# Two 57x64 blocks a score tile for the second half of the heads, u's first stage in 64-row halves, and a new written-out order

## The chip, the cores and the metric

The kernel runs on one core of a Trainium2 chip. The metric is the device time of one execution in microseconds. An execution's span, in the profile, goes from the first to the last instruction; the execution's own time is a little longer. The engines are PE (TensorE's matmuls, with their weight loads as PEld), DVE (VectorE), ACT (ScalarE), POOL (GpSimd) and SP, which here issues most DMAs. Each works through its own queue in order.

## The reference

Inputs are bf16; S = 2048 positions, D = 640 channels, H = 32 heads of 20. The result is a gated sum of two branches.

```python
x = A_q
g = sigmoid((x * gate_w).sum(-1, keepdims=True))
# A: a 4-tap causal filter on k, times v, then a causal convolution over all S positions by FFT
kv = k_shift * v
y  = irfft(rfft(kv, 2*S) * rfft(ssm_k, 2*S))[:S] + kv * ssm_D
a  = q * y
# B: attention of each position to the 8 positions 0, 2, .., 14 behind it
idx = pos[:, None] - 2 * arange(8)[None, :]
o = softmax(mask(q . k[idx] * scale)) . v[idx]
b = o @ wo
out = g * a + (1 - g) * b
```

## The kernel before

**Order.** Every part of the kernel is a Python generator (a stream) that yields one request at a time: a PE unit that takes PSUM, an eviction on ACT or DVE, a DMA on SP, something on POOL. The string `ORDER` names the stream that goes next, one letter a request (with `-`, the other of the two engines that a request allows). So all five instruction queues are written out by hand in one table; the waits between engines follow from the data. PSUM is four double banks; a unit takes one or two of them, and its eviction gives them back.

**Attention.** Positions are split into even and odd ones, so the 8 keys of a query are neighbours. A parity has 9 blocks of `BQ` = 114 queries, with `BK` = 121 keys each: 18 blocks. Four heads share a step t (8 steps), in four 32-row strips of `kb` and `qb`, which hold 20 features and 11 mask rows that push scores outside the band far down. `score_gen` makes scores with keys on partitions and queries on columns (L647, a 31x128 weight tile and 114 columns), and ACT takes the exponential of two heads and 3 or 4 blocks at a time out of PSUM into `ETall` (L658), a ring of `NET` = 9 tiles. `pv_gen` multiplies (L682): the weights are `ETall`, the moving side is V with a column of ones (`VW`), 21 columns a head; three heads are streamed (63 columns) though only the first counts, the next matmul overwrites the rest. DVE divides by the sum (L692, L694) and writes to `oS`, which lies in `VW`. From t = 6 on some pad matmuls (L652) follow the scores. `vproj` makes V (L526), half of the heads each; `qkproj` makes q and k (L573), which reach `kb` and `qb` by DMA.

**Convolution.** Two halves P of the channels, 40 channels a group of partitions. `transform` runs for h (the kernel) and u (k times v, in the tile `vin`, made by `conv` and `conv_v` on DVE): ten units of a first stage (`s1_unit`; h has two 64-row matmuls of 128 columns a channel, L713; u has one 128-row matmul of 256 columns against a block diagonal matrix, L709), each evicted as 1024 columns, then eleven units of a second stage (`s2_unit`, L732), evicted in place as 960 or 640 columns. u's tile `UC` is allocated (`u_slot`) where attention's buffers lay, so u's first stage starts when attention is done. `swaps` makes, by DMA, a copy `Hw` of h with the halves of the partitions exchanged: per P four steps of two DMAs, each step after a tiny POOL copy (L822) that waits until the step before has landed. `products` multiplies u with h and with `Hw` on DVE (L764, 44 instructions), `inverse1` is the inverse's first stage (L843), `final` its second (L930).

**End.** `op_tr` transposes `oS` (L861, 18 a unit, 5 units) into `oT`, which takes `vin`'s place; `outproj` multiplies it with `wo` (L877), 32 units; ACT scales them by 1 - g into `bl` (L891); DVE puts everything together and SP writes it out. The evictions of all stages go through `copy` (L244 on ACT, L246 on DVE).

Of the kernel before, what the change touches and what calls it, by code (L numbers as in the profile page):

```python
# [27 lines left out]
BK = 121  # L28
NBP = 9
# [10 lines left out]
NET = 9  # L40
GROUPS = [[0, 1, 2, 3], [4, 5, 6, 7], [8, 9, 10, 11], [12, 13, 14], [15, 16, 17]]
PARTS = [((0, 1, 2), 0, 2), ((3, 4), 12, 1)]
# [174 lines left out]
def kernel(  # L217
# [41 lines left out]
    ident = p0.tile([128, 128], BF, name="ident")  # L259
    F = p0.tile([128, 512], BF, name="F")  # L260
# [30 lines left out]
    ETall = pR.tile([128, NET, 2, 3 * BQ + 128], BF, name="ETall")  # L291
# [106 lines left out]
    def heads():  # L398
# [33 lines left out]
        nc.vector.memset(ETall[:, :, :, 3 * BQ:], 1.0)  # L432
        for q in range(4):
            nc.gpsimd.memset(kin[32 * q:32 * q + 1, 0:3, :], 0.0)
        for e in range(3):
            masks(e)

# [81 lines left out]
    def vproj(hp):  # L519
        for j in range(NBP):  # L520
            for par in range(2):
                g = yield Req("P", 0.0, xdeps(BQ * j - PRE, BQ * j - PRE + BK) + [ev(f"Wv{hp}")], take=1, half=1, pe=(5, 136.0, 272.0, 126.0))
                ps = psum(g)
                s0 = X0 + HP * par + BQ * j - PRE
                for dt in range(NDT):
                    nc.tensor.matmul(ps[0:BK, 0:320], lhsT=xT[:, dt, s0:s0 + BK], rhs=Wv[:, dt, 320 * hp:320 * hp + 320],  # L526
                                     start=(dt == 0), stop=(dt == NDT - 1))
                r = yield Req("AD", n=320, deps=[g.done], give=g.banks)
                copy(r.eng, VW[0:BK, NBP * par + j, 16 * hp:16 * hp + 16, 0:DH], ps[0:BK, 0:320].rearrange("p (h d) -> p h d", d=DH))
# [107 lines left out]
    def score_gen():  # L637
        s = 0
        for t in range(NT):
            kb, qb = ksets[t % 3], qsets[t % 3]  # L640
            for gi, blocks in enumerate(GROUPS):
                nb = len(blocks)
                g = yield Req("P", 0.0, [ev(f"set{t}")] + ([ev(f"near{t}")] if t < 2 else []), take=2, pe=(4 * nb, 11.8, 30.0, 11.8))
                for bb, b in enumerate(blocks):
                    for h4 in range(4):
                        r = 32 * h4
                        nc.tensor.matmul(psum(g, h4 // 2)[:, h4 % 2, BQ * bb:BQ * bb + BQ], lhsT=kb[r:r + DH + NF, BK * b:BK * b + 128],  # L647
                                         rhs=qb[r:r + DH + NF, BQ * b:BQ * b + BQ],
                                         start=True, stop=True, tile_position=(r, 0), skip_group_check=True)
                w = 512 - BQ * nb  # L650
                for n in range(0 if t < 6 else (2 if nb == 3 else (14 if t == 6 else 7))):
                    nc.tensor.matmul(psum(g, 1)[:, 1, BQ * nb:512], lhsT=mm[:, 0:128], rhs=mm[:, 0:w], start=True, stop=True, skip_group_check=True)  # L652
                if gi == len(GROUPS) - 1:
                    mark(f"sc{t}", g)
# [338 lines left out]
```

## Time and profile before

| | |
|---|---|
| time, 3 runs | 221.22 us median (220.27 to 222.21) |
| profiled execution | 219.82 us, span 218.0 us |
| mean granted TensorE clock | 0.990 |
| PE busy (modelled) | 205.2 us, 94% |
| DVE busy | 183.4 us, 84% |
| ACT busy | 173.5 us, 80% |
| DMA | 33.35 MB, mean 153 GB/s |

Matmuls are pipelined and their ends are modelled, so PE's busy share overstates how full PE is; how long a run of matmuls really holds PE is read from the chain of waits, which gives start and length of each run.

### The profile page before, as it was taken

How to read it: one execution, taken by the hardware profiler on the slowest of the kernel's cores; microseconds unless marked ns; L12 is line 12 of the kernel's file. 1: busy time of each engine (PE TensorE's matmuls, PEld its weight loads, DVE VectorE, ACT ScalarE, POOL GpSimd, SP SyncE). 2: the span in 40 equal slices, each digit the busy share in tenths (PEclk: the TensorE clock that was granted, in tenths of full speed). 3: DMA queues.
4: the chain of work that ended last, by engine and by line, in shares of the span. 5: the costliest groups of instructions: out<-in, count | busy, mean ns of one | idle time of the engine just before them, and what ended most of it. 6: DMA issues, size and time to landing. Idle time of an engine off the chain costs nothing.

```text
span 218.0 us, 8528 instructions
## 1 busy us (share of the span) xinstructions
PE 205.2 (94%) x3642; PEld 166.8 (76%) x3642; DVE 183.4 (84%) x264; ACT 173.5 (80%) x251; POOL 50.8 (23%) x129
## 2 busy tenths in 40 slices
PE   6999999999999999999997988999999999999990
PEld 3876987696677677656685766899888999998880
DVE  6647778997998998789897968998999997898782
ACT  0354387769998998989998988999899999487760
POOL 7980811460517045405420000000000000000000
PEclk9999999999999999999999699999999999999999
DMA  6999799699954993899984196767449064003544
GB/s 199 349 251 287 205 185 188 137 168 154 272 160 102 150 146 64 152 150 151 168 160 107 31 223 140 174 158 226 110 110 289 7 149 95 3 3 96 139 128 131
DMA packets 69049, 33.35 MB, mean 153 GB/s; under 512 B 51476, under 2 KB 66708, under 8 KB 69012
## 3 DMA queue, kind: packets, MB, share of 16 engines
q1 hardware_dynamic: 65684, 27.66, 62.0%
q0 software_dynamic: 2880, 4.90, 9.6%
q8 instruction: 28, 0.46, 1.0%
q10 hardware_dynamic: 448, 0.26, 0.4%
q14 instruction: 9, 0.07, 0.1%
HBM read 19.51 MB, written 2.62 MB: 102 GB/s over the span
## 4 chain that ended last, share of the span: by engine, by line
PE 66%; DVE 12%; ACT 6%; SPq 6%; DMA 5%; issue 3%; DVEq 0%; ACTq 0%
PE PS L573 16%; PE PS L526 12%; PE PS L877 10%; PE PS L843 8%; ACT ETall L658 5%; PE PS L682 5%; SPq L324 5%; PE PS L647 4%; PE PS L732 3%; DVE UC L246 3%; DMA h_lin<-in_A_ssm_k_dram 3%; DVE SX L246 3%; PE PS L930 2%; DMA WvT<-in_B_wqkv_dram 2%; PE PS L444 2%
## 5 line engine op out<-in xcount | busy, mean ns | idle before, releaser
L658 ACT ACTIVATE ETall<-PS 121x912 bf16<-121x912 f32 (+1 forms) x80 | 63.9, 865 | 6.4 <-PE PS L647 6.0
L573 PE MATMUL PS<-xT,Wqk 128*128 128x342 bf16 (+1 forms) x300 | 49.8, 310 | 0.7 <-ACT stg L244 0.3
L244 ACT CAST UC<-PS 128x1024 bf16<-128x1024 f32 (+2 forms) x49 | 44.4, 1030 | 4.0 <-DVE UC L246 3.1
L573 PEld LDWEIGHTS <-Wqk 128*128 128x128 bf16 x300 | 27.3, 97 | 14.6 <-issue 0.5
L526 PE MATMUL PS<-WvT,xT 128*121 128x320 bf16 x180 | 27.5, 301 | 0.6 <-DMA WvT<-in_B_wqkv_dram 0.3
L472 DVE TENSOR_TENSOR KX<-KX 128x1280 bf16<-128x1280 bf16 x32 | 25.3, 820 | 0.3
L526 PEld LDWEIGHTS <-xT 128*121 128x121 bf16 x180 | 23.5, 134 | 2.2 <-issue 0.4
L623 POOL DMA_DIRECT2D qb<-stg x29 | 14.5, 504 | 43.3 <-ACT stg L244 27.1
L877 PE MATMUL PS<-wo,oT 128*128 128x320 bf16 x160 | 24.5, 302 | 0.1
L244 ACT CAST stg<-PS 128x363 bf16<-128x363 f32 (+1 forms) x39 | 17.1, 472 | 8.5 <-PE PS L573 8.2
L877 PEld LDWEIGHTS <-oT 128*128 128x128 bf16 x160 | 21.0, 145 | 1.5 <-issue 0.5
L623 POOL DMA_DIRECT2D kb<-stg x36 | 18.0, 510 | 14.8 <-ACT stg L244 7.6
L732 PEld LDWEIGHTS <-G 64*128 64x128 bf16 x512 | 18.1, 93 | 3.8 <-issue 2.5
L682 PEld LDWEIGHTS <-ETall 121*128 121x128 bf16 x576 | 17.8, 97 | 1.6 <-issue 0.2
L682 PE MATMUL PS<-VW,ETall 121*128 121x63 bf16 (+2 forms) x576 | 18.5, 186 | 0.1
L843 PE MATMUL PS<-F,Hw 128*128 128x128 bf16 x160 | 18.1, 219 | 0.0
L843 PEld LDWEIGHTS <-Hw 128*128 128x128 bf16 x160 | 17.9, 114 | 0.0
L647 PE MATMUL PS<-qb,kb 31*128 31x114 bf16 x576 | 15.6, 212 | 2.3 <-ACT ETall L658 1.2
L246 DVE CAST UC<-PS 128x1024 bf16<-128x1024 f32 x13 | 15.3, 1220 | 2.6 <-ACT UC L244 1.2
L647 PEld LDWEIGHTS <-kb 31*128 31x128 bf16 x576 | 9.3, 93 | 10.3 <-issue 8.8
L246 DVE CAST SX<-PS 128x1024 bf16<-128x1024 f32 (+2 forms) x13 | 14.6, 1159 | 2.8 <-PE PS L732 1.7
L891 ACT ACTIVATE bl<-PS,omg 128x320 bf16<-128x320 f32 x30 | 15.4, 566 | 1.9 <-PE PS L877 1.4
(75 smaller groups left out, 329.9 us busy)
## 6 DMA issues: line engine op xcount, KB each, us to landing
xn<-in_A_q_dram SPq DMA_DIRECT2D x8, 320.0 KB
h_lin<-in_A_ssm_k_dram SPq DMA_DIRECT2D x16, 160.0 KB
vin<-in_A_v_dram SPq DMA_DIRECT2D x8, 320.0 KB
Hw<-H SPq DMA_DIRECT2D x8, 320.0 KB
q<-in_A_q_dram SPq DMA_DIRECT2D x8, 320.0 KB
Hw<-SX SPq DMA_DIRECT2D x8, 320.0 KB
kb<-stg POOLq DMA_DIRECT2D x28, 85.1 KB, 4.1
out_dram<-q SPq DMA_DIRECT2D x16, 120.0 KB
```

What stands on the lines that cost most here:

```text
L244: nc.scalar.copy(dst, src)
L246: nc.vector.tensor_copy(dst, src)
L472: eng.tensor_tensor(d, kin[:, n + 3 - j:n + 3 - j + m, :], w.to_broadcast([128, m, QC]), ALU.mult)
L526: nc.tensor.matmul(ps[0:BK, 0:320], lhsT=xT[:, dt, s0:s0 + BK], rhs=Wv[:, dt, 320 * hp:320 * hp + 320], start=(dt == 0), stop=(dt == NDT - 1))
L573: nc.tensor.matmul(ps[:, 0:n], lhsT=Wqk[:, dt, w, 128 * ft:128 * ft + 128], rhs=xT[:, dt, s0:s0 + n], start=(dt == 0), stop=(dt == NDT - 1))
L623: (nc.sync if near else nc.gpsimd).dma_start(dst[r0:r0 + rows, 0:wd], stg[fa - f0:fb - f0, 0:wd])
L647: nc.tensor.matmul(psum(g, h4 // 2)[:, h4 % 2, BQ * bb:BQ * bb + BQ], lhsT=kb[r:r + DH + NF, BK * b:BK * b + 128], rhs=qb[r:r + DH + NF, B ...
L658: nc.scalar.activation(ETall[0:BK, e, :, 0:BQ * nb], psum(g, k)[0:BK, :, 0:BQ * nb], ACT.Exp, scale=SCALE)
L682: nc.tensor.matmul(O[:, (b - b0) // 6, c0:c0 + 21 * nh], lhsT=ETall[0:BK, e, hh, BQ * bb:BQ * bb + 128], rhs=VW[0:BK, b, 4 * t + h4:4 * t ...
L732: nc.tensor.matmul(ps[:, c, 160 * jj:160 * jj + 160], lhsT=G[rows, j0 + jj, 64 - 64 * rr:192 - 64 * rr], rhs=Am[rows, rr].rearrange("p o ( ...
L843: nc.tensor.matmul(d, lhsT=st[(key, P)][:, c, o + il // 4, :, il % 4], rhs=M[:, k, :], start=(k == 0), stop=(k == 1), skip_group_check=True)
L877: nc.tensor.matmul(op, lhsT=oT[:, ft].rearrange("p h m a -> p a (h m)")[:, t, :], rhs=wo[:, ft, 320 * n:320 * n + 320], start=(ft == 0), s ...
```

## The change

What it does, in eight parts:

1. For steps t = 4 to 7 (`NEW` = 4) a block of 114 queries becomes two of `SQ` = 57 queries with `SK` = 64 keys each, one in the lower and one in the upper 64 partitions of the score tile. A score matmul has a 32x64 weight tile and 57 columns; there are twice as many, and an ACT exponential holds two heads and six blocks, 128x684. A step has three score groups in place of five, so 24 exponentials replace 40.
2. `pv_gen` for these steps has two matmuls a head and block, each with a 64x64 tile on the diagonal of the array and 21 columns.
3. `vproj` for the second half of the heads makes V in the same two row halves: two matmuls with a 128x64 tile in place of one with 128x121.
4. All exponentials are stored with 64 columns per 57 queries, so `ETall` has 8 tiles instead of 9. Fewer and wider pad matmuls stand behind the last scores (24, not 71).
5. u's first stage works as h's does: two 64-row matmuls of 128 columns a channel. For P = 0 it writes to a tile of its own, `UA`, which is there before attention ends; its second stage evicts from `UA` into `UC`.
6. `oT` moves into `UA`'s place, and the copy `Hw1` for P = 1 into `vin`'s place, so its swap now waits for u's first stage of both halves.
7. `op_tr` transposes against `pick`, a matrix that also drops the doubled rows, and has an extra transpose of 8 rows for each parity, 20 a unit.
8. `ORDER` is another table from the first third on.

```diff
-NET = 9
-GROUPS = [[0, 1, 2, 3], [4, 5, 6, 7], [8, 9, 10, 11], [12, 13, 14], [15, 16, 17]]
+NET = 8
+GROUPS = [[[0, 1, 2, 3], [4, 5, 6, 7], [8, 9, 10, 11], [12, 13, 14], [15, 16, 17]],
+          [[0, 1, 2, 3, 4, 5], [6, 7, 8, 9, 10, 11], [12, 13, 14, 15, 16, 17]]]
...
 ORDER = """
-dddii-iddifd-iifxdddxedidffdfddefcicccii-iddiedd-icddlie-iiiyf-yddccdixiyyfy-xe-ydddexixdxddyyfyy-xcccxxffccccccccciiiciiccdcii
+-iidddii-iddifd-iifxdddxedidffdfddefcicccii-iddiedd-icddlie-iiiyf-yddccdix-icydydcccfcccifceccfcccdcccccxyicyycixiedi-ydfd-xiciy
...
@@ vproj @@
+                    for i in range(2 if split else 0):
+                        nc.tensor.matmul(ps[SK * i:SK * i + SK, 0:320], lhsT=xT[:, dt, s0 + SQ * i:s0 + SQ * i + SK], rhs=rhs,
+                                         start=(dt == 0), stop=(dt == NDT - 1), tile_position=(0, SK * i), skip_group_check=True)
...
@@ score_gen @@
+                    for i in range(1 + split):
+                        for h4 in range(4):
+                            r = 32 * h4
+                            c, q = BK * b + SQ * i, BQ * b + SQ * i
+                            nc.tensor.matmul(psum(g, h4 // 2)[SK * i:SK * i + SK, h4 % 2, bw * bb:bw * bb + bw] if split else psum(g, h4 // 2)[:, h4 % 2, bw * bb:bw * bb + bw],
+                                             lhsT=kb[r:r + DH + NF, c:c + (SK if split else 128)], rhs=qb[r:r + DH + NF, q:q + bw],
+                                             start=True, stop=True, tile_position=(r, SK * i), skip_group_check=True)
-                for n in range(0 if t < 6 else (2 if nb == 3 else (14 if t == 6 else 7))):
+                for n in range(0 if t < 6 else (((5 if t == 6 else 3)) if split else (2 if nb == 3 else (14 if t == 6 else 7)))):
...
@@ pv_gen @@
-                                nh = min(3, 4 - h4)
+                                nh = min(1 if split else 3, 4 - h4)
+                                for i in range(1 + split):
+                                    rows = slice(SK * i, SK * i + SK) if split else slice(0, BK)
...
+                                                     start=True, stop=True, tile_position=(SK * i, SK * i), skip_group_check=True)
...
@@ s1_unit @@
-            if whole:
-                nc.tensor.matmul(ps[:, il // 2, 256 * (il % 2):256 * (il % 2) + 256], lhsT=vin[:].rearrange("p c n i -> p i (c n)")[:, i], rhs=F1d,
-                                 start=True, stop=True, skip_group_check=True)
-            for qp in range(0 if whole else 2):
+            for qp in range(2):
                 rows = slice(64 * qp, 64 * qp + 64)
+                lhsT = vin[rows].rearrange("p c n i -> p i (c n)")[:, i] if key == "u" else h_lin[rows, i - PL * P, :, :].rearrange("p c n -> p (c n)")
...
@@ transform @@
-        Am = st[(key, P)]
+        early = key == "u" and P == 0
+        Am = st["UA"] if early else st[(key, P)]
...
+        if early:
+            yield Req("N", 0.0, [ev("p3")])
+        Bm = st[(key, P)]
...
@@ swaps @@
-            yield Req("N", 0.0, outs("h", P) + [ev("p2")])
+            yield Req("N", 0.0, outs("h", P) + ([ev("us10"), ev("us11")] if P else [ev("p2")]))
...
@@ op_tr @@
-            for b in range(NB):
-                par, j = b // NBP, b % NBP
-                w = min(BQ, HS - BQ * j)
-                nc.tensor.transpose(tr[:, par, BQ * j:BQ * j + w], oS[0:w, b, 128 * ft:128 * ft + 128], ident[0:w, 0:w])
+            for par in range(2):
+                for j in range(NBP - 1, -1, -1):
...
+                    nc.tensor.transpose(tr[:, par, q:q + k], oS[0:k, NBP * par + j, feats], pick[0:k, c:c + k])
+                nc.tensor.transpose(tr[:, par, BQ:BQ + 8], oS[0:8, NBP * par + 1, feats], ident[0:8, 0:8])
```

How the order moves work shows at three places. Lines have other numbers in the changed kernel: the exponential is L680, `copy` L248 and L250, the swaps L859.

On ACT, from the last third of attention to the first evictions of the outer projection, before (`SX` is h of P = 1, `UC` is u, `ETall` the exponentials, `bl` the projection):

```order
L658 ACTIVATE ETall<-PS 121x2x456 x6
L244 CAST SX<-PS 128x2x512 x4
L658 ACTIVATE ETall<-PS 121x2x342 x4
L658 ACTIVATE ETall<-PS 121x2x456 x6
L658 ACTIVATE ETall<-PS 121x2x342 x4
L244 CAST SX<-PS 128x80x12 x4
L244 CAST UC<-PS 128x2x512 x12
L244 CAST UC<-PS 128x80x12 x11
L891 ACTIVATE bl<-PS,omg 128x320 x2
```

The same place on ACT in the changed kernel:

```order
L680 ACTIVATE ETall<-PS 128x2x6x57 x4
L248 CAST H_301<-PS 128x80x12
L248 CAST SX<-PS 128x2x512
L680 ACTIVATE ETall<-PS 128x2x6x57 x2
L248 CAST UA<-PS 128x2x512
L680 ACTIVATE ETall<-PS 128x2x6x57 x2
L248 CAST SX<-PS 128x2x512
L680 ACTIVATE ETall<-PS 128x2x6x57 x2
L248 CAST SX<-PS 128x2x512 x2
L248 CAST UA<-PS 128x2x512
```

The exponentials are fewer, h's second half is less far when they end, and u's first stage (`UA`) stands partly among them; the rest of it follows mixed with h's stages.

On SP, from the last swap of P = 0 on, before (`Hw` are the swaps of h, `wo` the outer projection's weights, the second `SX` the table T, q the gated input):

```order
L904 DMA q_2428<-in_A_q_dram 32x8x640
L828 DMA Hw<-H_289 64x5x512 x2
L828 DMA Hw<-SX 64x5x512 x2
L324 DMA wo<-in_B_wo_dram 128x5x640
L828 DMA Hw<-SX 64x5x512 x6
L324 DMA SX<-cf_T 128x4x512 x2
```

And in the changed kernel:

```order
L859 DMA Hw_2980<-H_301 64x5x512 x7
L329 DMA wo<-in_B_wo_dram 128x5x640
L859 DMA Hw_2980<-H_301 64x5x512
L859 DMA Hw_3695<-SX 64x5x512 x8
L938 DMA q_3370<-in_A_q_dram 32x8x640 x3
```

`wo` now stands ahead of the last swap of P = 0, all eight swaps of P = 1 behind it, and every load of q behind the swaps.

On PE, `op_tr` between two parities, before:

```order
L861 MATMUL PS<-ident,VW 128x114
L861 LDWEIGHTS VW
L861 MATMUL PS<-ident,VW 128x112
L861 LDWEIGHTS VW
L861 MATMUL PS<-ident,VW 128x114
```

And in the changed kernel:

```order
L894 LDWEIGHTS VW
L894 MATMUL PS<-pick,VW 128x121
L895 LDWEIGHTS VW
L895 MATMUL PS<-ident,VW 128x8
L894 LDWEIGHTS VW
L894 MATMUL PS<-pick,VW 128x120
```

A transpose of 8 rows now stands between transposes of up to 122 rows; in the built program its tile is 32 rows by 128 columns, while that of its neighbours is 128 by 128.

More of the change, by code (lines that the diff above doesn't have):

```diff
@@ L28 @@
 BK = 121
+SQ = 57
+SK = 64
+NEW = 4
 NBP = 9
@@ L259 @@
     ident = p0.tile([128, 128], BF, name="ident")
+    pick = p0.tile([128, 3 * BK], BF, name="pick")
     F = p0.tile([128, 512], BF, name="F")
@@ L290 @@
         ksets.append(kb); qsets.append(qb)
-    ETall = pR.tile([128, NET, 2, 3 * BQ + 128], BF, name="ETall")
+    ETall = pR.tile([128, NET, 2, 8 * SK], BF, name="ETall")
     rds = []
@@ L431, in heads @@
             nc.gpsimd.memset(xT[:, :, X0 + HP * c + HS:X0 + HP * (c + 1)], 0.0)
-        nc.vector.memset(ETall[:, :, :, 3 * BQ:], 1.0)
+        nc.vector.memset(ETall[:].rearrange("p e h (c q) -> p (e h c) q", q=SK)[:, :, SQ:], 1.0)
         for q in range(4):
@@ L436, in heads @@
             masks(e)
+        runs, c = [(0, SQ), (SK, SQ), (SQ, 7)], 0
+        for k in (BK + 1, HS - BQ * (NBP - 1) + 8):
+            runs += [(SQ, 7), (k - 1, 1), (0, SQ), (SK, k - SK - 1)]
+        for r, w in runs:
+            nc.gpsimd.tensor_copy(pick[:, c:c + w], ident[:, r:r + w])
+            c += w
     def xpose():
@@ L640, in score_gen @@
             kb, qb = ksets[t % 3], qsets[t % 3]
-            for gi, blocks in enumerate(GROUPS):
+            split = t >= NEW
+            bw = SQ if split else BQ
+            for gi, blocks in enumerate(GROUPS[split]):
                 nb = len(blocks)
-                g = yield Req("P", 0.0, [ev(f"set{t}")] + ([ev(f"near{t}")] if t < 2 else []), take=2, pe=(4 * nb, 11.8, 30.0, 11.8))
+                g = yield Req("P", 0.0, [ev(f"set{t}")] + ([ev(f"near{t}")] if t < 2 else []), take=2, pe=(4 * nb * (1 + split), 11.8, 30.0, 11.8))
@@ L658, in score_gen @@
-                    nc.scalar.activation(ETall[0:BK, e, :, 0:BQ * nb], psum(g, k)[0:BK, :, 0:BQ * nb], ACT.Exp, scale=SCALE)
+                    r = yield Req("A", 68.0 + 0.834 * 2 * bw * nb, [g.done, etfree[e], ev("ET")], give=[g.banks[k]])
+                    nc.scalar.activation(ETall[0:rows, e].rearrange("p h (c q) -> p h c q", q=SK)[:, :, 0:bw * nb // SQ, 0:SQ],
+                                         psum(g, k)[0:rows, :, 0:bw * nb].rearrange("p h (c q) -> p h c q", q=SQ), ACT.Exp, scale=SCALE)
@@ L702, in s1_unit @@
     def s1_unit(key, P, oc, Am):
-        whole = key == "u"
-        r = yield Req("P", 0.0, [], take=1, pe=(4, 109.0, 220.0, 106.7) if whole else (8, 25.5, 70.0, 26.7))
+        r = yield Req("P", 0.0, [], take=1, pe=(8, 25.5, 70.0, 26.7))
         ps = psum(r)
@@ L787, in p2_slot @@
         st["p2"] = ctx.enter_context(tc.tile_pool(name="p2", bufs=1, side="left", reuse_waits="tile"))
-        for P in range(2):
-            Hw = st["p2"].tile([128, 2, 10, 128, 4], BF, name="Hw", tag=f"Hw{P}")
-            st[("w", P)] = Hw
+        UA = st["p2"].tile([128, 2, 10, 128, 4], BF, name="UA", tag="UA")
+        Hw = st["p2"].tile([128, 2, 10, 128, 4], BF, name="Hw0", tag="Hw0")
+        st["UA"], st[("w", 0)] = UA, Hw
         mark("p2", g)
@@ L813, in swaps @@
         for P in range(2):
-            yield Req("N", 0.0, outs("h", P) + [ev("p2")])
+            yield Req("N", 0.0, outs("h", P) + ([ev("us10"), ev("us11")] if P else [ev("p2")]))
+            if P:
+                Hw1 = p0.tile([128, 2, 10, 128, 4], BF, name="Hw1", tag="V")
+                st[("w", 1)] = Hw1
             Hs = st[("h", P)]
```

96 lines of the change are left out of this document (49 added, 47 removed).

## The prediction

> **What bounds the kernel now.** First the page's busy times, then the stages. The span of the profiled execution is 218.0 us, its time 219.82, so 1.8 us lie around the span; it is 1.4 us below the median of the runs, 221.22.
>
> ```profile
> span 218.0 us, 8528 instructions
> PE 205.2 (94%) x3642; PEld 166.8 (76%) x3642; DVE 183.4 (84%) x264; ACT 173.5 (80%) x251; POOL 50.8 (23%) x129
> PE 66%; DVE 12%; ACT 6%; SPq 6%; DMA 5%; issue 3%; DVEq 0%; ACTq 0%
> ```
>
> PE has two thirds of the chain that ended last, but no engine is far from full. The order of the two kernels is the same for the first 62 us, so I cut the rest into four stages: to the end of `conv_v` and `qkproj` (A), to the end of u's first stage (B), to the last product (C), and the end (D).
>
> ```profile
> core 0: us, PE busy (x) PEld busy (x) DVE busy (x) ACT busy (x) POOL busy (x), PEclk, DMA share, GB/s
> 62.50:111.50 49.00, 48.05 (x874) 34.74 (x874) 43.88 (x62) 44.96 (x70) 19.20 (x52) 1.00 0.91 134
> 111.50:150.50 39.00, 35.00 (x731) 29.89 (x728) 33.40 (x37) 36.14 (x44) 0.76 (x4) 0.96 0.64 147
> 150.50:182.50 32.00, 31.81 (x550) 29.06 (x549) 31.55 (x52) 31.06 (x42) 0.37 (x2) 1.00 0.59 145
> 182.50:213.50 31.00, 30.35 (x793) 27.80 (x790) 26.11 (x41) 22.45 (x34) 0.00 (x0) 1.00 0.28 73
> ```
>
> In A PE is idle 0.95 us of 49, in C 0.2 of 32, in D 0.65 of 31. B is the stage with air: PE idle 4.0 of 39, ACT and DVE busy 69.5 of 78 together. Its waits show who is late:
>
> ```profile
> 118.19 0.22 PE L647 MATMUL PS<-qb,kb 31*128 31x114 bf16 x2 [0.25 <-ACT ETall L658]
> 119.10 0.38 PE L647 MATMUL PS<-qb,kb 31*128 31x114 bf16 x14 [0.69 <-DVE SX L246]
> 121.34 2.49 PE L713 MATMUL PS<-F,h_lin 64*128 64x128 bf16 x40 [0.42 <-ACT ETall L658]
> 120.00:130.00 10.00, 8.93 (x217) 7.18 (x214) 7.95 (x9) 8.83 (x12) 0.19 (x1) 0.83 0.59 121
> ```
>
> PE waits for exponentials and evictions to give PSUM back, and after that thin stretch the granted clock is 0.83 from 120 to 130 us: 10 x 0.17 = 1.7 us of clock lost, that is 3.4 us at half rate.
>
> **The change part by part.** Exponentials.
>
> ```profile
> L658 ACT ACTIVATE ETall<-PS 121x912 bf16<-121x912 f32 x48 | 41.9, 944 | 2.1 <-PE PS L647 1.9
> L658 ACT ACTIVATE ETall<-PS 121x684 bf16<-121x684 f32 x32 | 22.1, 745 | 4.3 <-PE PS L647 4.1
> ```
>
> Removed for t = 4 to 7: 24 x 0.944 + 16 x 0.745 = 34.6 us; added: 24 of 684 columns, 24 x 0.745 = 17.9 us. ACT loses **16.7 us**, half of it in A and half in B (20 of the 40 lie in each). Other evictions change sides a little: counted by the order, ACT gets some 2 us back and DVE gives 1 up. DVE's total work thus stays; that is why the 16.7 us don't come through whole. In A PE has 0.95 us of air, and all of it is the most that can come: **-1.0**. In B ACT and DVE share the evictions: 69.5 - 8.3 = 61.2 us, or 30.6 each; B was 39.0 for 34.75 each, so 4.1 shorter at best. PE's own work there is about 31 + u's; I take four fifths, 3.3, since the engines still wait for each other, and half of the clock's 1.7 us, as u's and h's matmuls now stand among the scores: **-4.2**. Bounds: 0 to -5.8.
>
> Second product (`pv_gen`) and scores. The trace has no 64x64 and no 32x64 tile. The nearest rows are the weight loads and the runs of small tiles:
>
> ```profile
> L526 PEld LDWEIGHTS <-xT 128*121 128x121 bf16 x180 | 23.5, 134 | 2.2 <-issue 0.4 <-DVE xT L246 0.4
> L709 PEld LDWEIGHTS <-vin 128*128 128x128 bf16 x80 | 9.1, 161 | 1.2 <-issue 0.8
> L682 PEld LDWEIGHTS <-ETall 121*128 121x128 bf16 x576 | 17.8, 97 | 1.6 <-issue 0.2
> L930 PEld LDWEIGHTS <-SX 32*32 32x32 bf16 x512 | 4.4, 88 | 2.0 <-issue 1.6
> 36.45 1.30 PE PS L682 x48
> ...
> 58.69 0.37 PE PS L647 x16
> ...
> 64.65 0.55 PE PS L713 x16
> ...
> 93.98 1.19 PE PS L539 x20
> ...
> 148.66 1.93 PE PS L709 x16
> ...
> 193.66 0.96 PE PS L930 x96
> ```
>
> A load of 32 columns takes 88 ns, one of 121 columns 134: 0.52 ns a column, so about 17 ns of the 88 are columns and 71 fixed. A full load of 128 columns takes only 97, some 26 ns beyond the fixed part: it goes faster than its columns. A 64-column load at the slow rate holds its tile 33 ns. L713 shows two tiles side by side: 34 ns a matmul of 128 columns, where L709's 256 columns take 120. So two diagonal tiles give 33 / 2 = 16.5 ns a matmul: 576 x 16.5 = 9.5 us against 288 x 1.30 / 48 = 7.8. **+1.7**, of which about half lies under B's idle PE: +0.9. Bounds: 10 ns each as in L930 (-2.0), 36 ns if the tiles load one after the other (+12.9). Scores: 576 at L930's 10 ns are 5.8, against 288 x 0.37 / 16 = 6.7; I take 0, bounds -0.9 and +2.8 (16.5 ns).
>
> [...]
>
> `vproj`. L539 runs four column tiles of 512 columns in 4 x 60 = 238 ns, side by side; two of 320 columns then take what one took. 0; one after the other they would be 90 x 0.136 = +12.2, which that row speaks against.
>
> u's first stage. Before 80 x 0.12 = 9.7 us (L709). Its weights lie 160 bytes apart and take 161 ns to load, 64 more than `ETall`'s, so about 161 - 71 = 90 ns of columns; 64 rows have as many columns. Two halves side by side are then held by the load, not by the 69 ns of an L713 pair: I take 100 ns a channel, 8.0 us: **-1.6**. Bounds: 69 ns (-4.1), two loads in turn, 180 ns (+4.7). The evictions stay 20 of 1024 columns.
>
> `op_tr`. PE pays for a change between full array and row tiles:
>
> ```profile
> 63.12 0.86 PE PS L573 x5
> 63.97 0.68 PE PS L526 x5
> ...
> 66.61 0.27 PE PS L647 x12
> 66.88 0.82 PE PS L526 x5
> 67.70 0.72 PE PS L573 x5
> ```
>
> The same five matmuls take 0.68 us behind other full-array ones and 0.82 behind scores: 0.14 to come back, and I take 0.1 to leave. The ten 8-row transposes stand on a 32-row tile between full ones: 10 x 0.24 = **+2.4** on PE in C, where it has no air. Bounds 0 (if such a tile doesn't count as a change) and 3.
>
> At nothing: the 47 fewer pads, which filled PE where it waited anyway; POOL's eleven copies for `pick`, which lie ahead of the first fragments that POOL waits for (without that cover each would cost what L822's small copies show in the trace, well under a microsecond in all); the ring of 8 tiles, whose tile now holds six blocks instead of four, so that it reaches further back than 9 did.
>
> Sum: -1.0 - 4.2 + 0.9 - 1.6 + 2.4 = **-3.5 us**. On the profiled execution 219.82 - 3.5 = 216.3, on the median 221.22 - 3.5 = **217.7**.
>
> **What waits anew.** `Hw1` lies where `vin` lay, so P = 1's swap starts after u's first stage.
>
> ```profile
> POOL Hw L822 <- DMA Hw<-H: 26.3, 3, 11.1
> POOL Hw L822 <- DMA Hw<-SX: 10.4, 2, 5.3
> 170.02 0.66 DVE L764 TENSOR_TENSOR SX<-UC,SX 128x960 bf16<-128x960 bf16 x1
> ```
>
> A step lasts 5.2 us undisturbed and up to 11.1. Before, that stage ended at 150.5; with the part of it that stands in attention and the gain of A and B, I estimate 143. Four steps from there end at 164; P = 1's first product came at 170.0 and would come some 4 us earlier. Cover: 2 us. Behind that product all of DVE's queue waits (evictions of the inverse, gating, `final`), and q's loads wait behind the swaps on SP.
>
> **The rivals.** *The idle goes altogether.* The relief of 16.7 us lets PE fill B with u's second stage, and the load of u is as fast as h's: all of -5.8 in A and B and another 0.9 of clock, u -4.1, product -2.0 x 1/2, `op_tr` +2.4: about -9, 212. For: ACT and DVE bound B. Against: DVE stays as full as before, 108.8 of 120 us up to the last product.
>
> *Nothing comes of it.* Either the swap is late by what was won (a step or two near 11 us, as at 116 to 137 us, eat the cover and 4 us), or small matmuls keep a floor. [...] L930's 10 ns a matmul disagrees for rotating tiles; L682's 27 doesn't tell. A floor near L682's own 27 ns gives 576 x 27 = 15.6, +7.8, half of it hidden: -3.5 - 0.9 + 3.9 = -0.5, 220.7.
>
> *Slower:* tiles load one after the other. Product +12.9, u +4.7 instead of -1.6; of these 17.6 us B hides its 4.0 of idle PE, and nothing hides the rest: -3.5 - 0.9 + 1.6 + 13.6 = +10.8, 232. It decides from about 7 us on, that is from some 26 ns a matmul of the second product with u's loads in turn. A half of it (226) is likelier than the whole. For: the slow loads. Against: in L647 four row tiles come at 23 ns each, less than a load lasts.
>
> **How the numbers follow.** The forecast's own case, 215 to 219: 0.40. The idle gone, under 215: 0.20. Nothing, 219 to 223.4: 0.24. Slower, over 223.4: 0.16. A measurement of this kernel tells about 1% from no change. So faster 0.60, same 0.24, slower 0.16. The range leaves a tenth on each side: 212 to 224.5.
>
> **What would show it.** In the profile after: 24 exponentials of 128x684 near 0.75 us; the second product's 48 matmuls in a run of about 0.8 us (0.5 and 1.7 are the rivals); eight of u's in about 0.4 us (0.28 and 0.72); `op_tr`'s units some 0.5 us longer than 18 transposes would be; B with a granted clock near 1.00 and less idle PE; POOL's waits for the swap short of the first product of P = 1. Wrong I'd be if DVE, not PE, waited in C, or if the clock fell again among the 21-column matmuls.

## The result, and the profile after

The changed kernel takes 242.74 us (median of 4 runs, 240.98 to 242.93) against 221.47 for the kernel before: ratio 1.0948, 95% interval 1.0877 to 1.102. Forecast were 217.7 and a range of 212 to 224.5. A few disturbed runs are left out of all ratios below.

The page of the profile after, lines as they answer to those of before (span, busy times, the queue q8, the chain that ended last), and then the line of q8 before:

```profile
span 240.5 us, 9930 instructions
PE 216.2 (90%) x4351; PEld 171.0 (71%) x4351; DVE 181.1 (75%) x263; ACT 164.0 (68%) x236; POOL 58.0 (24%) x140
q8 instruction: 34, 0.56, 1.1%
PE 69%; ACT 8%; DMA 8%; DVE 7%; issue 5%; SPq 1%; POOL 0%; DVEq 0%; ACTq 0%
```

```profile
q8 instruction: 28, 0.46, 1.0%
```

ACT lost work, 9.5 us (173.5 to 164.0) where some 15 were forecast, and DVE 2.3; and yet PE's busy time grew by 11 us and "issue" in the chain from 3% of 218 us to 5% of 240.5. The same four stages A to D as in the prediction, at their new ends and with its columns (busy us of PE, PEld, DVE, ACT and POOL, then granted clock, DMA share and GB/s):

```profile
64.70:118.50 53.80, 50.28 (x1021) 32.41 (x1020) 42.03 (x58) 37.39 (x59) 16.75 (x47) 0.94 0.87 135
118.50:162.10 43.60, 38.32 (x1264) 32.63 (x1261) 32.96 (x38) 34.67 (x42) 3.05 (x9) 0.92 0.40 95
162.10:204.40 42.30, 36.66 (x581) 33.44 (x579) 33.57 (x54) 34.70 (x45) 6.00 (x3) 0.96 0.65 133
204.40:236.00 31.60, 28.95 (x756) 26.38 (x756) 25.43 (x40) 18.64 (x27) 0.00 (x0) 0.94 0.38 96
```

A and B together last 97.4 us in place of 88.0, C 42.3 in place of 32, D 31.6 in place of 31. The remaining 2.2 us are lost before 62 us, where both orders are the same: there the granted clock (the share of its full rate that the profile lists for PE, here always 0.5 or 1.0) was first full at 10.1 us in this execution and at 5.5 in that of before; the kernels below have it full from 4.5 to 10.1 us. So two stretches have to be explained: some 9 us before u's first stage ends, some 10 us behind it.

The first, in the chain by time on PE:

```profile
104.25 0.76 PE L590 MATMUL PS<-xT,Wqk 128*128 128x349 bf16 x4
104.94 0.57 PE L668 MATMUL PS<-qb,kb 31*64 31x57 bf16 x48
105.44 1.70 PE L712 MATMUL PS<-VW,ETall 64*64 64x21 bf16 x96
107.07 0.30 PE L668 MATMUL PS<-qb,kb 31*64 31x57 bf16 x24
110.07 0.39 PE L668 MATMUL PS<-qb,kb 31*64 31x57 bf16 x24 [2.70 <-issue]
...
139.94 1.56 PE L712 MATMUL PS<-VW,ETall 64*64 64x21 bf16 x87
143.21 0.39 PE L712 MATMUL PS<-VW,ETall 64*64 64x21 bf16 x9 [1.71 <-issue]
```

PE stops in the middle of a unit, twice, and no semaphore is named (`issue`). About each stop the granted clock goes to half for 6.8 us (from 109.1 and from 143.2 us). What answers is the queue that the page lists as q8, by its count PE's instructions: PE has 2 x 4351 matmuls and weight loads, 34.0 times 256, and q8 34 packets of 16,384 bytes (before, 28.5 and 28). So a packet is a block of 256 instructions of 64 bytes. In the records of this queue one packet begins at 100.27 us and the next only at 107.30, when PE has used up 511 instructions since, and PE goes on 1.6 us after that packet's end. PE had run out of instructions.

The second stretch, DVE's rows in order of time and then POOL's:

```profile
175.81 0.65 DVE L792 TENSOR_TENSOR H<-UC,H 128x960 bf16<-128x960 bf16 x1 
...
185.31 0.48 DVE L792 TENSOR_TENSOR Hw<-UC,Hw 128x640 bf16<-128x640 bf16 x1
192.12 0.66 DVE L792 TENSOR_TENSOR SX<-UC,SX 128x960 bf16<-128x960 bf16 x1 [6.33 <-issue]
```

```profile
174.37 0.19 POOL L853 COPY Hw<-Hw 128x1 bf16<-128x1 bf16 x1 [5.39 <-DMA Hw<-SX]
180.68 5.16 POOL L853 COPY Hw<-Hw 128x1 bf16<-128x1 bf16 x1 [6.13 <-DMA Hw<-SX]
```

DVE stands for 6.33 us before the first product of P = 1, which waits for the last step of the swap. That step stands behind a POOL copy of one element a partition that took 5.16 us in place of 0.19: it ended at 185.84 us, when DVE was through with the products of P = 0 (185.79), which had run one after the other since 175.81.

### The profile page after: what moved, and what is told of

It reads as the page before. It is cut to its first block, busy times and chain, and to the rows that moved or that the text cites. A ratio compares the mean times of both kernels' runs of the same rounds, so it can differ in the third digit from the quotient of the medians.

```text
span 240.5 us, 9930 instructions
## 1 busy us (share of the span) xinstructions
PE 216.2 (90%) x4351; PEld 171.0 (71%) x4351; DVE 181.1 (75%) x263; ACT 164.0 (68%) x236; POOL 58.0 (24%) x140
## 4 chain that ended last, share of the span: by engine, by line
PE 69%; ACT 8%; DMA 8%; DVE 7%; issue 5%; SPq 1%; POOL 0%; DVEq 0%; ACTq 0%
PE PS L590 18%; PE PS L756 7%; PE PS L911 7%; PE PS L712 6%; PE PS L541 6%; PE PS L543 6%; PE PS L874 6%; DMA q<-in_A_q_dram 5%; PE PS L668 4%; PE PS L740 4%; PE PS L894 2%; ACT ETall L680 2%; ACT UC L248 2%; DMA WvT<-in_B_wqkv_dram 2%; PE PS L964 2%
## 5 line engine op out<-in xcount | busy, mean ns | idle before, releaser
L680 ACT ACTIVATE ETall<-PS 121x912 bf16<-121x912 f32 (+2 forms) x64 | 49.8, 829 | 10.4 <-PE PS L668 8.9
L248 ACT CAST UC<-PS 128x1024 bf16<-128x1024 f32 (+2 forms) x40 | 37.7, 1011 | 10.6 <-PE PS L874 10.5
L640 POOL DMA_DIRECT2D qb<-stg x29 | 14.5, 504 | 42.8 <-ACT stg L248 18.9
L248 ACT CAST stg<-PS 128x363 bf16<-128x363 f32 (+1 forms) x35 | 15.6, 461 | 13.0 <-PE PS L590 10.9
L250 DVE CAST stg<-PS 128x342 bf16<-128x342 f32 (+1 forms) x25 | 13.0, 526 | 12.9 <-PE PS L590 10.9
L712 PEld LDWEIGHTS <-ETall 64*64 64x64 bf16 (+1 forms) x864 | 19.3, 108 | 3.9 <-issue 2.5
L712 PE MATMUL PS<-VW,ETall 64*64 64x21 bf16 (+3 forms) x864 | 20.5, 180 | 1.8 <-issue 1.7
L853 POOL COPY Hw<-Hw 128x1 bf16<-128x1 bf16 x6 | 6.6, 1096 | 58.3 <-DMA Hw<-H 33.1
L668 PE MATMUL PS<-qb,kb 31*64 31x57 bf16 (+1 forms) x864 | 15.2, 204 | 3.5 <-issue 2.7
L668 PEld LDWEIGHTS <-kb 31*64 31x64 bf16 (+1 forms) x864 | 10.2, 101 | 10.5 <-issue 9.0
L248 ACT CAST VW<-PS 128x320 bf16<-128x320 f32 (+1 forms) x25 | 10.8, 430 | 9.7 <-PE PS L543 5.4
L250 DVE CAST UC<-PS 128x1024 bf16<-128x1024 f32 (+2 forms) x12 | 13.9, 1172 | 2.7 <-ACT UC L248 1.1
```

Source lines behind the costliest of these rows:

```text
L248: nc.scalar.copy(dst, src)
L250: nc.vector.tensor_copy(dst, src)
L640: (nc.sync if near else nc.gpsimd).dma_start(dst[r0:r0 + rows, 0:wd], stg[fa - f0:fb - f0, 0:wd])
L668: nc.tensor.matmul(psum(g, h4 // 2)[SK * i:SK * i + SK, h4 % 2, bw * bb:bw * bb + bw] if split else psum(g, h4 // 2)[:, h4 % 2, bw * bb:bw ...
L680: nc.scalar.activation(ETall[0:rows, e].rearrange("p h (c q) -> p h c q", q=SK)[:, :, 0:bw * nb // SQ, 0:SQ], psum(g, k)[0:rows, :, 0:bw * ...
L712: nc.tensor.matmul(O[out, (b - b0) // 6, cs], lhsT=ETall[rows, e, hh, q0:q0 + (SK if split else 2 * SK)], rhs=VW[rows, b, 4 * t + h4:4 * t ...
```

## Experiments

The theories are *instructions* (PE uses them up faster than they are fetched, and the clock falls behind the stops) and *late swap*; against both stand *the new order* (work is in the wrong places) and *the tiles themselves*. Times of different kernels are compared as ratios to the kernel before, with 95% intervals.

**The swap in one go** (`ungated`).

```diff
-                        nc.gpsimd.tensor_copy(Hw[:, c, o, 0, 0:1], Hw[:, lc, lo, 0, 0:1])
+                        if P == 0:
+                            nc.gpsimd.tensor_copy(Hw[:, c, o, 0, 0:1], Hw[:, lc, lo, 0, 0:1])
```

> The changed kernel, but the four steps of the swap of P = 1 go out in one go: the one-element copies on POOL between them are left out, and nothing else differs. In the changed kernel that swap began at 162.2 us, its last step was issued at 187 (after a copy that lasted 5.16 us), and P = 1's first product came at 192.1 behind 6.3 us of idle DVE. Theory 'late swap': with all 2.6 MB in flight at once they land near 177, the products of P = 1 follow those of P = 0 without a gap, and the 6.3 us, part of PE's wait for the last product (5.2 us) and of its half clock after it (3.4 us) go: 233 to 237 us. Theory 'PE runs out of instructions' says nothing of this stretch: the gaps at 107 and 141 us stay. Rival 'the swap is hidden anyway, the later stages are late by themselves': 241 to 243.

235.75 us, ratio 1.0643 (1.0577 to 1.0709). DVE's rows, now without a gap:

```profile
185.44 0.49 DVE L792 TENSOR_TENSOR Hw<-UC,Hw 128x640 bf16<-128x640 bf16 x1
185.84 0.65 DVE L792 TENSOR_TENSOR SX<-UC,SX 128x960 bf16<-128x960 bf16 x1
```

The late swap is shown: 1.0948 - 1.0643 = 3.05% of the time before, 6.7 us. Why POOL's copy lasted so long is read from times alone, but from several kernels: five that swap at the changed kernel's place have a copy that starts among products that run one after the other (5.16 us here, 5.24 in `wide`, 5.36 in `no_h1_load`, 5.40 in `dense_tail`, 6.52 in `nosplit`), and each ends within 0.1 us of the last of them. Where DVE copied `oT` out of PSUM between the products, such a copy took 0.19 us (159.4 us in the kernel before, 175.9 in `split_only`).

**More columns a matmul** (`wide`), **and both** (`ungated_wide`).

```diff
-                                nh = min(1 if split else 3, 4 - h4)
+                                nh = min(3, 4 - h4)
```

> The changed kernel, but each matmul of the split second product streams up to three heads' columns (63, 42 or 21, as in the kernel before) in place of 21; what is too much is overwritten by the next heads. The number of instructions stays, the rate at which PE uses them up falls. Theory 'PE runs out of instructions': the unexplained gaps of 2.70 us at 107 and 1.71 us at 141 shrink to under 1 us and the half clock behind them goes (2 x 3.4 us), against some 576 x 10 ns = 6 us more streaming: 238 to 243, and the stretch up to the end of u's first stage no longer than 162. Rival 'the gaps come from the tiles themselves (a drain between kinds of tiles)': the gaps stay and the streaming adds up: 246 to 250.

> The swap of P = 1 in one go and the second product of up to 63 columns together. If the two losses are separate, -7.0 and -1.3 add up: 233 to 236. If the swap then only waits longer for u's first stage, or the clock falls elsewhere, no better than the swap alone: 235 to 238.

241.40 us (ratio 1.0867, 1.0788 to 1.0947) and 233.15 (1.0554, 1.048 to 1.063): a small gain, clear of the uncertainty in neither pair alone. The added columns cost PE nothing: a run of 96 lasts 1.70 us in `ungated_wide`, with up to 63 columns (106.91 us), as with 21 (105.44 above), so streaming isn't what holds a 64x64 tile. The stops get shorter but stay (1.33 and 1.43 us in `wide`, 1.74 and 1.98 in `ungated_wide`), as the instructions are the same; half clock before 160 us is 10.2 us in both, in place of 13.7 and 20.5.

**Six more pads** behind the scores of t = 4 and 5 (`ungated_pads`).

```diff
-range(0 if t < 6 else (((5 if t == 6 else 3)) if split
+range(0 if t < 4 else (((6 if t < 6 else 5 if t == 6 else 3)) if split
```

> The swap of P = 1 in one go, and six pad matmuls of 170 columns more behind each group of scores of t = 4 and 5, 36 in all, as they stand for t = 6 and 7 already: by the row of those some 0.13 us each, 4.7 us more work for PE, which nobody reads. Theory 'PE runs out of instructions, and the clock falls where PE then stands still': they slow the use of instructions and fill PE where it waits; less half clock before 160 us than the 20 us it had with the swap alone, and the time at most as long: 231 to 236. Rival 'PE's work sets the time there': 4 to 5 us longer, 239 to 241.

238.79 us (ratio 1.0816, 1.0699 to 1.0932), with 27 us of half clock before 160 us in place of 20. The theory that pads would hold the clock missed: they cost 3.8 us, most of the 4.7 that they were estimated to take.

**The fetch by itself** (`dense_tail`).

```diff
+    for n in range(768):
+        r = slice(64 * (n % 2), 64 * (n % 2) + 64)
+        nc.tensor.matmul(PS[r, 0, 0, 0:21], lhsT=ident[r, 0:64], rhs=F[r, 0:21], ...)
+    ... 768 more with 63 columns, the eight transfers, 1536 more with 21
```

> The changed kernel with three blocks of matmuls added behind its last work, which nothing reads: 768 on two diagonal 64x64 tiles of 21 columns with no transfer under way, 768 of 63 columns, then 1536 of 21 columns while eight transfers in pieces of 128 bytes (h's rows, loaded once more) run beside them. Only these blocks are looked at, not the time. Theory 'PE runs out of instructions': a matmul and its weight load are two instructions, blocks of 256 instructions (16 KB) are fetched as PE uses them up, and 17 ns a matmul use up 128 of them in 2.2 us, less than a fetch lasts; so the first block shows a stop at about every 128th matmul and lasts nearer 20 than 13 us, the second (27 ns or more a matmul, 3.5 us for 128) stops little, and the third stops longer as long as the transfers run (4 to 5 us for 128). Rival 'the stops come from attention's waits or from changes of tile': no stops, 13, 21 and 26 us.

PE's rows in the second and the third block, and then a stretch of each block (PE busy behind the length, granted clock third from the end):

```profile
264.27 2.21 PE L1005 MATMUL PS<-F,ident 64*64 64x63 bf16 x128 [1.52 <-issue]
268.00 2.21 PE L1005 MATMUL PS<-F,ident 64*64 64x63 bf16 x128 [1.52 <-issue]
271.72 2.21 PE L1005 MATMUL PS<-F,ident 64*64 64x63 bf16 x128 [1.52 <-issue]
283.46 3.59 PE L1013 MATMUL PS<-F,ident 64*64 64x21 bf16 x128 [0.96 <-issue]
288.01 21.13 PE L1013 MATMUL PS<-F,ident 64*64 64x21 bf16 x768 [0.96 <-issue]
```

```profile
237.00:254.00 17.00, 15.13 (x546) 14.84 (x548) 0.00 (x0) 0.00 (x0) 0.00 (x0) 0.50 0.02 5
261.00:275.50 14.50, 8.71 (x516) 8.27 (x510) 0.00 (x0) 0.00 (x0) 0.00 (x0) 1.00 0.02 5
279.00:288.00 9.00, 7.08 (x256) 6.88 (x256) 0.00 (x0) 0.00 (x0) 0.00 (x0) 0.50 0.90 120
```

With nothing else under way, at full clock, PE stops after every 128th matmul, that is after 256 instructions: 2.21 us of work, 1.52 of standing, **3.73 us a block of 256**. No wait and no change of tile size is in there. The expectation had the blocks the wrong way round: the 63-column ones run at full clock, 17 ns each, and so stop long; the 21-column ones run at half clock, 28 ns each, and hardly stop (0.41 us behind 256 of them). Beside transfers in pieces of 128 bytes a block takes 3.59 + 0.96 = 4.55 us, at half clock. In these blocks the clock follows neither PE's busy share (0.89 of the first stretch, at half; 0.60 of the second, at full) nor the stops; what differs is the columns. That isn't all of it: `nosplit`, below, has half clock without any 64x64 tile.

In attention, from 60 to 170 us, eleven of the kernels have stops named `issue` of over 0.6 us, 23 in all. Every one ends 1.3 to 2.1 us behind the end of a q8 packet. The kernel before, `thin`, `uhalf`, `nosplit` and `new_fewer` have none. So these stops are the fetch.

**The same without h's transfers** (`no_h1_load`).

```diff
+                if P:  # a request without a transfer in place of the load
+                    ...
+                    continue
```

> The changed kernel without the eight transfers that bring h's rows of P = 1 (1.3 MB in pieces of 128 bytes, from 99.9 to 113.5 us in the changed kernel); its result for P = 1 is then computed from P = 0's rows. Looked at for the stretch from 100 to 125 us, not for the time. If these transfers hold up the fetch of instructions, the block of 256 that was due near 105 us comes in time or half as late: PE's stop of 2.70 us at 107 falls below 1.5 us, and the half clock from 109 us on goes or is shorter. If the fetch is late by itself (3.4 to 3.7 us a block without any transfer), the stop stays near 2 us or more.

PE's rows where the changed kernel stood for 2.70 us:

```profile
103.58 1.70 PE L718 MATMUL PS<-VW,ETall 64*64 64x21 bf16 x96
105.21 0.30 PE L674 MATMUL PS<-qb,kb 31*64 31x57 bf16 x24
107.38 0.30 PE L674 MATMUL PS<-qb,kb 31*64 31x57 bf16 x24 [1.87 <-issue]
```

It stops at the same matmul, for 1.87 us, with 3.4 us of half clock in place of 6.8. By this one profile of each the transfers make 0.8 us of the stop; the rest is the fetch's own.

**The split taken back in the new order** (`nosplit`).

```diff
-NEW = 4
+NEW = 8
 ORDER: for t = 4 to 7 three more score letters behind the second and the third group
```

> The changed kernel with the split of attention alone undone: heads 16 to 31 on 18 blocks of 114 queries again, 40 exponentials in place of 24 for them, the order kept, with the added scores and exponentials right behind those that they go with. u's halves, the swap's place and op_tr stay. Theory 'PE runs out of instructions': no unexplained gap over 0.5 us and no half clock from 100 to 150 us; some 9 us come back up to the end of u's first stage, less what of ACT's 17 us shows there (up to 8): 232 to 241, with the wait for P = 1's swap as it was. Rival 'it is the order: the work stands in the wrong places': 243 and more, the stretch to the end of u's first stage as long as before or longer.

246.49 us (ratio 1.1125, 1.1059 to 1.119). No stop without a cause is left, as *instructions* had it, but PE waits for exponentials (4.7 us from 60 to 165 us) and for evictions on DVE (2.2) instead, and the clock is at half for 20.5 us from 131.7 us on. The total speaks for the rival; it says that this order needs ACT's 17 us, and can't tell more, since sixteen exponentials were pressed into places made without them.

**The split alone in the old order** (`split_only`; everything of u, the swap and `oT` as before), and the same with up to 63 columns (`split_wide`, `nh` as in `wide`).

```diff
 ORDER: that of the kernel before; for t = 4 to 7 the letters of the second and the fourth of five score groups go
-        early = key == "u" and P == 0
+        early = False
 ... s1_unit, p2_slot, u_stream, swaps and oT's place as before
```

> The split of attention (with vproj's, the new row layout of oS and op_tr's extra transposes) in the order of the kernel before: of the scores' five pairs for heads 16 to 31 the three that stay stand where the first, third and fifth stood. u's first stage, the places of Hw1 and oT and all of the rest are those of the kernel before. The prediction's terms for attention and op_tr alone: -1.0, some -3.5 of B, +0.9 and +2.4 make -1.2, 219 to 221. Theory 'the new order and the late swap cost the time': the same, 217 to 221. Theory 'PE runs out of instructions and its clock falls wherever the small tiles stand densely': unexplained gaps and half clock between 100 and 145 us here too, up to 10 us: 223 to 231.

> The split of attention in the order of the kernel before, as in the run of that, but with up to 63 columns a matmul in the split second product. The number of PE's instructions is the same. With 21 columns that kernel had 20.5 us more at half clock than the kernel before had between 60 and 160 us (3.4 us there), which costs some 10 us, and 6.8 us of unexplained stops of PE. If the clock falls because 21-column matmuls stream too little, even while PE stands busy, half or more of those 10 us come back: 226 to 233, with the stops still there. If the clock falls only behind the stops: they stay and so does it, 236 to 240 (more streaming). If the stops were all and the clock nothing: as before, 235 to 238.

237.33 us (ratio 1.0741, 1.0656 to 1.0825) and 236.24 (1.0656, 1.0565 to 1.0747). PE's longest waits in `split_only` from 60 to 170 us:

```profile
PE PS L762 <- issue: 3.8, 1, 3.8
PE PS L668 <- issue: 3.0, 3, 1.8
```

So neither the new order nor the late swap is needed for a loss of 16 us. With up to 63 columns the mean granted clock of the runs is 0.947 to 0.974 in place of 0.938 to 0.956, and the time hardly less: the first of the three readings falls.

**Thin matmuls in the kernel before** (`thin`).

```diff
-                                nh = min(3, 4 - h4)
+                                nh = 1
```

> The kernel before with one number changed: each matmul of the second product streams one head's 21 columns in place of up to three heads' 63, so less work for PE, the same number of instructions, no split. If thin matmuls draw the clock down by themselves, half clock appears between 36 and 140 us, where the kernel before has 3.4 us of it, and the time is no shorter: 221 to 229. If PE pays for streaming alone (up to 10 ns less on 576 matmuls, part of it beside waits): 217 to 220, clock as before. If the weight loads set 27 ns and the clock follows waits alone: the same time, 220 to 222.

Ratio 0.9974 (0.9938 to 1.001). The clock falls as the first reading says, 10.2 us at half from 120 to 135 us in place of 3.4, and here it costs nothing: PE is busy for 18.47 us from 120 to 140 in place of 17.84, so it takes up idle time. That doesn't tell what half clock costs where PE has none.

**u's halves alone** (`uhalf`).

```diff
-        whole = key == "u"
+        whole = False
+        ... lhsT = vin[rows].rearrange("p c n i -> p i (c n)")[:, i] if key == "u" else ...
```

> The kernel before with u's first stage in 64-row halves and nothing else of the change (80 matmuls of 256 columns become 160 of 128; the same order, the same evictions with h's pattern). The prediction had -1.6 us (219.9), bounds -4.1 and +4.7. The changed kernel's trace now shows 0.46 to 0.54 us for eight of them, where four of the whole ones took 0.48: by that row 0, 220.5 to 222.5. If the loads went in turn: 226.

Ratio 0.999 (0.9948 to 1.0032). PE does get faster, 16 matmuls in 0.86 us where L709 took 0.96 for the same eight channels, and then stands:

```profile
145.51 0.86 PE L713 MATMUL PS<-F,vin 64*128 64x128 bf16 x16 [0.27 <-DVE UC L246]
146.64 3.12 PE L713 MATMUL PS<-F,vin 64*128 64x128 bf16 x56 [0.27 <-DVE UC L246]
```

**The added matmuls of attention taken away**: those of the second product (`split_fullpv`), those and the scores' (`split_fewer`), both in the new order with the swap in one go (`new_fewer`). Exponentials and evictions stand as they were. One full matmul in place of two halves mixes the halves' keys, and the scores of each block's second half are left out.

```diff
-for i in range(1 + split): nc.tensor.matmul(O[out, ...], lhsT=ETall[rows, e, hh, q0:q0 + SK], ...)
+nc.tensor.matmul(O[:, ...], lhsT=ETall[0:128, e, hh, q0:q0 + 2 * SK], ...)
-for i in range(1 + split): ... lhsT=kb[r:r + DH + NF, c:c + SK] ...
+... lhsT=kb[r:r + DH + NF, BK * b:BK * b + 128] ...
```

> The split of attention in the order of the kernel before (237.3 us), but its second product for heads 16 to 31 is done by one 128x128 matmul of up to 63 columns a block, as in the kernel before, in place of two 64x64 ones. That mixes the keys of the two halves: its values are not those of the reference; exponentials, evictions and everything else stand as they were. PE gets 288 matmuls, 576 instructions, fewer; the work by PE's own durations is 288 x 27 = 7.8 us in place of 576 x 17 = 9.8. If the number of instructions costs the time: half of the 1152 added ones go, and with them half or more of the 16 us: 224 to 231, the stops of over 1 us gone or fewer. If the tiles' own durations do: 2 us less, 234 to 236.

> As the run before, and the scores of heads 16 to 31 are one matmul of 128 keys by 57 queries a block and head in place of two of 64 by 57 (the second half's scores are those of the first half's queries; values again not the reference's). PE's instructions in attention are then as many as in the kernel before; the 24 exponentials of 684 columns in place of 40, vproj's halves, the new rows of oS and op_tr's extra transposes stay. If the number of instructions cost the 16 us, no stop of over 1 us is left and the prediction's terms for exponentials and op_tr show: -1.0 - 4.2 + 2.4 = -2.8, 216 to 221. If the tiles or the exponentials' new shape cost them: 232 to 236.

> The changed kernel in its own order with the swap of P = 1 in one go (235.8 us), and with the same two replacements in attention (values again not the reference's). If instructions cost what is left there, too: 216 to 222, without stops of over 1 us from 100 to 150 us and with less than 7 us of half clock before 160 us. If the new order costs time by itself (evictions or transfers too late for what stands behind them): 226 to 234.

230.16 (ratio 1.0449, 1.0384 to 1.0514), 227.66 (1.0325, 1.0269 to 1.0381) and 225.53 us (1.0254, 1.0181 to 1.0328). In both orders the added matmuls make about as much: 1.0741 - 1.0325 = 4.2% in the old (9.2 us), 1.0643 - 1.0254 = 3.9% in the new (8.6 us). But neither kernel comes down to the time before, as *instructions* alone had it. And these two kernels do less than the kernel before: with 57 columns a score matmul takes 11 ns, as 24 in 0.27 us show in `split_fewer`, where it took 23 with 114.

```profile
108.53 0.34 PE L666 MATMUL PS<-qb,kb 31*128 31x57 bf16 x24
108.80 0.59 PE L758 MATMUL PS<-H,G 64*128 64x160 bf16 x12
```

All 288 are 3.2 us in place of 6.7 before the change and of 576 x 10.4 ns = 6.0 with the split. So up to 2.8 us of the 8.6 are scores that the kernel before did too. The stretch from 100 to 150 us before the change, in the changed kernel, and in `new_fewer`, one after the other (busy PE, PEld, DVE, ACT and POOL, granted clock, DMA share, GB/s):

```profile
100.00:150.00 50.00, 45.49 (x958) 37.67 (x955) 43.99 (x50) 46.65 (x59) 7.72 (x18) 0.97 0.72 152
```

```profile
100.00:150.00 50.00, 43.01 (x1422) 33.40 (x1419) 33.00 (x44) 32.41 (x44) 7.35 (x16) 0.86 0.50 88
```

```profile
100.00:150.00 50.00, 43.29 (x1093) 35.25 (x1094) 42.17 (x51) 42.15 (x55) 6.93 (x16) 1.00 0.61 100
```

The clock is back at 1.00, and DVE and ACT get 84 us of work done there, where they did 65 in the changed kernel.

How much of the 8.6 us is the stops and how much the clock isn't settled. From 60 us to the last matmul of u's first stage PE is idle for 7.7 us in `ungated` (busy 94.35 of 102) and for 8.5 in `new_fewer` (82.69 of 91.2): where it no longer stops for instructions (3.5 us in place of 0.5) it waits for ACT and DVE. The difference lies in runs that last longer. By their lengths at full clock the added matmuls are 4 to 5 us of it (2.8 for the scores; 576 x 17 ns against 288 of 27 to 30 for the product, 1.2 to 2.0). The rest falls among the 20.5 us of half clock, which `new_fewer` doesn't have. In a dense run half clock and the fetch hide each other, since `dense_tail` takes 28 ns a pair at half clock, hardly stopping, and 29 at full clock with its stops; `ungated_wide`, with half as much half clock as `ungated`, is only some 2 us faster.

PE's two longest waits in `new_fewer` from 60 to 170 us:

```profile
PE PS L666 <- DVE VW L720: 2.3, 1, 2.3
PE PS L590 <- ACT stg L248: 1.6, 2, 0.9
```

In the old order ACT's relief ends at a transfer. PE's wait in `split_fewer`, and what DVE stood for before it:

```profile
122.69 1.21 PE L739 MATMUL PS<-F,h_lin 64*128 64x128 bf16 x16 [5.61 <-DVE h_lin L811]
```

```profile
122.12 0.52 DVE L811 TENSOR_TENSOR h_lin<-h_lin,Dz 128x80 bf16<-128x80 bf16 x1 [5.15 <-DMA h_lin<-in_A_ssm_k_dram]
```

## Why the prediction was wrong

From ratio to ratio, of 221.2 us: swap 6.7, added matmuls 8.6, the rest 1.0254 - 1 = 2.5% or 5.6; together the 21 us by which the kernel is slower. Each step has an uncertainty of some 2 us, and up to 2.8 us of the second belong to the rest, as said above. The sizes of single runs came out as forecast (exponentials of 128x684 in 758 ns, 48 matmuls of the second product in 0.86 us); what they cost in the kernel did not.

**Second product and scores: the term that failed most.** "So two diagonal tiles give 33 / 2 = 16.5 ns a matmul" is right within a run: 96 in 1.63 us from start to start are 17 ns, and 48 scores in 0.50 us 10.4. That a load of 64 columns goes at the slow rate, the source of the 33, was a choice between two rates; the trace after agrees, 103 to 110 ns a load (L712 from 105.4 us), near 71 + 33 = 104. The 16.5 isn't the sustained price. A matmul and its load are two instructions, and 3.73 us for 256 of them make 29 ns a pair in `dense_tail`, though the work takes 17. The change adds 288 matmuls to the product and 288 to the scores, 1152 instructions: 4.5 blocks, 16.8 us if all of them fell into dense runs. Measured are 8.6 and 9.2 (5.8 in the new order without the scores' 2.8), where +0.9 and 0 stood. The step that failed is to price a matmul by what holds its tile, and never to ask what feeds PE, though the q8 line of before could have told: 28 blocks in 218 us, one in 7.8 us on average. That the stops come from the fetch is shown; what half clock adds to the price stays open.

Two rivals had prices of this kind. "A floor near L682's own 27 ns" had the size, for the product alone and without a mechanism; it left the scores at 10 ns. *Slower*, with a chance of 0.16, had the direction by another mechanism, tiles that load one after the other, and runs of 17 ns speak against that. Its threshold is also too high: by its own terms 21 ns a matmul would do, not 26 (4.7 for u and 4.3 for the product, less 4.0 hidden and 2.8 won elsewhere, make the +2.2 us to 223.4).

**The swap: "Cover: 2 us".** Its start was estimated at 143 and its end at 164. u's first stage ended at 162.1, 11 us of that delay because of the step above (`new_fewer`: 151.2) and 8 because A and B won nothing, and the last of the four steps stood behind the copy of 5.16 us. The mechanism was named ("a step or two near 11 us"), its price is 6.7 us, and it came on top of the rest instead of in its place. "Nothing comes of it" had both causes as alternatives.

**A and B, -1.0 and -4.2.** They didn't come even with the added matmuls gone: `new_fewer` ends its last u matmul of the first stage at 151.2 us, before the change 150.6. ACT was relieved (46.65 to 42.15 us busy from 100 to 150), but PE got more idle (45.49 to 43.29 busy): it waits for DVE's division in attention and ACT's eviction of `stg`, the two lines above. In the old order h's rows of P = 1 end the wait (5.61 us). That transfer is also late: its requests go out from 102.3 to 117.1 us in `split_fewer`, from 99.4 to 111.6 before the change; why stays open. "Four fifths" of an engine average was a guess about what is late next, and that had not been looked up.

**u, -1.6.** PE's term was nearly right, 0.43 us a unit in `uhalf` against 0.48 before and the 0.40 forecast; the time is not, since the evictions ("stay 20 of 1024 columns") set this stage, as the waits of `uhalf` for DVE show (1.0 us in four).

**`op_tr`, +2.4.** Two units before the change, and what follows them:

```profile
150.47 1.98 PE L861 MATMUL PS<-ident,VW 114*128 114x114 bf16 x36
152.39 1.01 PE L732 MATMUL PS<-UC,G 64*128 64x160 bf16 x24
```

After it, the two kinds of transposes of one parity and the start of the next:

```profile
167.49 0.65 PE L894 MATMUL PS<-pick,VW 120*128 120x120 bf16 x9
168.07 0.17 PE L895 MATMUL PS<-ident,VW 8*128 8x8 bf16 x1
168.18 0.66 PE L894 MATMUL PS<-pick,VW 120*128 120x120 bf16 x9
```

A parity now takes 0.70 us from start to start, a unit 1.40; before, a unit took (152.39 - 150.47) / 2 = 0.96. 5 x 0.44 = 2.2 us: right in size. How much of it is the change of tile no row tells, since the nine full transposes got longer too. It is part of the 5.6 us of the rest. In the profiled executions (222.8 us against 218.0) that rest lies almost whole between the end of u's first stage and the first product of P = 1: there `new_fewer` loses 4.2 us to the kernel before (151.2 to 174.8 against 150.6 to 170.0). What else is in that stays open.

**What would make it wrong** was named: the clock did fall among the 21-column matmuls, and in C both DVE (6.3 us) and PE (5.2, for DVE's products) waited.

## What to carry to other kernels

Count PE's instructions as a resource: before splitting matmuls into shorter ones, divide the added instructions by 256, set up to 3.7 us (3.73 in `dense_tail`) against each such block in the stretch where they stand densely (here some 2 us a block came through), and look for idle PE with no releaser in the middle of a unit. A term of a sum that was won on one engine counts only up to the next wait, so look up which transfer or eviction comes due there. A tiny gating instruction can become the longest step of a chain when another engine is busy beside it (5.16 us for 0.19), so look at what runs at that time.

## What the runs showed of the hardware

- PE stops for instructions: 3.73 us for 256 with nothing else under way, 4.55 beside transfers of 128-byte pieces (there at half clock). All 23 stops of over 0.6 us in attention end 1.3 to 2.1 us behind the end of a packet of 256 instructions.
- The granted clock can be at half while PE is busy with hardly a stop (0.41 us behind 256 matmuls): 0.50 for 17 us of 21-column matmuls (PE busy 0.89), 1.00 for 14.5 us of 63-column ones (PE busy 0.60). In `thin`, where PE had idle time, 10.2 us at half cost nothing that shows.
- A run of 96 matmuls on two diagonal 64x64 tiles lasts 1.70 us with 21 columns and with up to 63; 128 with 63 take 2.21 us in `dense_tail`.
- A one-element POOL copy took 5.16 to 6.52 us in five kernels, until DVE's products were over, and 0.19 beside DVE's copies out of PSUM. The products read two tiles of SBUF, the copies out of PSUM none; whether that makes the difference isn't shown.
